# One weight matrix of a decode block loaded as two halves of its partitions, from two DMA queues

## The chip, the cores and the metric

The kernel runs on one core of a Trainium2 chip. A core has a matrix engine (TensorE, PE in the profile), a vector engine (VectorE, DVE), an engine for activation functions (ScalarE, ACT), a general engine (GpSimd, POOL) and one that mostly issues transfers (SyncE, SP). Sixteen DMA engines move data between the chip's main memory and the core's on-chip memory, which has 128 partitions. The metric is the time of one execution on the device in microseconds (us), as a median over runs; lower is better.

## What is computed

One decode step of a transformer block: a layer norm, then attention over a cache and a feed-forward layer beside each other, both added to the input. All data are 32-bit floats.

```python
B, Sq, D = 4, 1, 512
H, Sk, Dh = 32, 4096, 128        # F = 1792

def _A_ref(x, k_cache, v_cache, wq, wo):
    q = (x @ wq).reshape(B, Sq, H, Dh).transpose(0, 2, 1, 3)
    scores = jnp.einsum("bhqd,bhkd->bhqk", q, k_cache) * (Dh ** -0.5)
    p = _softmax(scores, axis=-1)
    o = jnp.einsum("bhqk,bhkd->bhqd", p, v_cache)
    return o.transpose(0, 2, 1, 3).reshape(B, Sq, H * Dh) @ wo

def _B_ref(x, w1, w2):
    h = _silu(jnp.einsum("bsd,df->bsf", x, w1))
    return jnp.einsum("bsf,fd->bsd", h, w2)

xn = _layernorm(x, axis=-1)
return x + _A_ref(xn, k_cache, v_cache, wq, wo) + _B_ref(xn, w1, w2)
```

The two caches are 4 x 32 x 4096 x 128 floats each, 268 MB apiece. wq is 512 x 4096 floats (8.39 MB), wo as large, w1 and w2 3.67 MB each.

## The kernel before

**Tiles and stages.** The caches are worked through in 32 tiles (`T`): one batch row and four heads at a time. A tile of K or V is 128 partitions x 128 rows x 128 floats, 64 KB in each partition, 8.39 MB in all. There are two buffers for K (`kb[0]`, `kb[1]`) and one for V (`v_t`).

**The start.** Before the first tile, w1 (line 196) and x (line 197) are loaded into `kb[0]`, wq (line 198) into `v_t`, and the first K tile, K(0), into `kb[1]` (line 199). The layer norm follows on x (lines 282 to 295, mostly DVE, the square root of line 288 on ScalarE), its transposes (lines 301 to 303), the first feed-forward product with w1 (line 312), the SiLU (line 322), its transposes into `hT` (lines 326 to 336), then the query product with wq: 64 matmuls recorded at line 348, whose first waits for wq's semaphore. Lines 359 to 371 rearrange the queries into `q_h`, and line 378 spreads them over the partitions.

**The loop.** For each tile DVE multiplies K by the spread queries (line 391) and, with GpSimd's help (line 422), sums the products into scores (lines 398 and 401); ScalarE takes exponentials (line 457); PE multiplies them with V (line 473); ScalarE copies the result out (line 466), GpSimd and PE gather it by heads (lines 431 to 439 and 483). After the last tile wo and w2 are multiplied in (lines 585 to 605), the result is copied and stored in two parts, one issued by SyncE and one by ScalarE (line 616).

**What sets the order.** The program is written out by hand: every engine has its own list of instructions, and semaphores order them. SyncE's list is one queue of loads: w1, x, wq, K(0), then K(1), which waits for the transposes of line 326 because `kb[0]` holds w1 and x until then, V(0), which waits for line 348 because `v_t` holds wq, and from there K(t+1) and V(t) in turn. K(t+1) waits for `k_free`, raised when the scores of two tiles before are done with the buffer, and V(t) for `v_free`, raised when PE has done with the V tile before. The last V tile goes into a K buffer; wo follows V in `v_t`, and w2 follows K in `kb[0]`. A DMA raises its semaphore by 16 when all of it has landed.

**Names that matter.** `load` (line 165) issues a load from SyncE, lets it raise a semaphore by 16 and gives back the pair of semaphore and count that a user waits for; `d_wq` is that pair for wq. The view `src` of wq puts four rows of the matrix, 64 KB, into each of the 128 partitions, and `wq_t` is the same shape in `v_t`.

Of the kernel before, what the change touches and what calls it, by code (L numbers as in the profile page):

```python
# [22 lines left out]
def kernel(  # L23
# [30 lines left out]
    P = nc.NUM_PARTITIONS  # L54
# [19 lines left out]
    PE, DVE, ACT, POOL, SP = nc.tensor, nc.vector, nc.scalar, nc.gpsimd, nc.sync  # L74
# [9 lines left out]
    sem = tc.alloc_semaphore  # L84
# [41 lines left out]
    wq_t = v_t.rearrange("p (c m) d -> p c (m d)", c=DC)  # L126
# [38 lines left out]
    def load(dst, src, s, *deps):  # L165
        inst = SP.dma_start(dst, src)
        for d, n in deps:
            inst.wait_op(d, n, "sem-ge", check=False)
        inst.then_inc(s, 16)
        return (s, 16)  # L170
# [19 lines left out]
    def load_k(t, *deps):  # L190
        load(kb[(t + 1) % 2], cache_tile(k_cache, t), k_landed[(t + 1) % 2], *deps)
# [3 lines left out]

    d_w1 = load(w1_t, w1.rearrange("(p c) f -> p c f", p=P), sem("w1"))
    d_x = load(x_sb, xf, sem("x"))
    d_wq = load(wq_t, wq.rearrange("(p c) n -> p c n", p=P), sem("wq"))
    load_k(0)


# [24 lines left out]
    rows = ident.rearrange("p (g n) -> p n g", g=G)  # L226
# [93 lines left out]
    for j in range(4):  # L320
        part_rows, n = slice(32 * j, 32 * j + B), FN[j] * P
# [20 lines left out]
    for m in range(NM):  # L342
        for c in range(DC):
            for j in range(4):
                n = NM * j + m
# [256 lines left out]
    for e, eng in enumerate((SP, ACT)):  # L602
# [9 lines left out]
        for k, j in enumerate((2 * e, 2 * e + 1)):  # L612
            c = acc[32 * j : 32 * j + B, :]
# [40 lines left out]
```

## Time and profile before

| | us |
|---|---|
| median of 3 runs | 1302.58 (1302.27 to 1302.63) |
| the profiled execution | 1302.57 |
| its span | 1300.8 |

| engine | busy us | share of the span |
|---|---|---|
| PE, matmuls | 401.0 | 31% |
| DVE | 912.0 | 70% |
| ACT | 99.8 | 8% |
| POOL | 576.4 | 44% |

The profile is one execution, taken by the hardware profiler. Its page gives busy times, the span in 40 slices of 32.5 us, the DMA queues, the chain of work that ended last, groups of instructions by source line, and DMA issues. A digit in a row of slices is the busy share in tenths, 9 meaning 90% or more; the rows "DMA" and "GB/s" are the mean busy share of the 16 DMA engines and what they moved. The timeline has one row for an instruction or a merged run of them: start, duration, engine, line, operation, output from input with shapes, count, and in brackets how long the engine had been idle and what released it. An engine's name with a q (SPq) is its sequencer, which issues DMAs and handles waits. The tensors are named by their buffers: `k<-in_B_w_dram` is w1 at the start (w2 at the end) going into a K buffer, `v<-in_A_wq_dram` is wq going into the V buffer. Windows give busy times, the granted TensorE clock, the DMA share and GB/s for chosen stretches of the span.

### The profile page before, as it was taken

What the parts mean: (1) busy time and instruction counts of PE and PEld (TensorE: products, weight loads), DVE (VectorE), ACT (ScalarE), POOL (GpSimd) and SP (SyncE); (2) the same over time, 40 slices, a digit from 0 to 9 for tenths busy, and PEclk for the clock granted to TensorE, in tenths of its full rate; (3) what the DMA queues carried; (4) which work ended last, traced back from release to release, by engine and by line L of the source; (5) the groups of instructions that cost most, each with busy time, mean ns of one, the idle gap of its engine ahead of it and who ended that gap; (6) DMA issues with size and microseconds to landing.
All of it is one profiled execution on the core that took longest, in us unless ns stands there. A gap on an engine that the chain in (4) does not pass through costs nothing. (4 is left out here: it accounts for less than half of the span.)

```text
span 1300.8 us, 6793 instructions
## 1 busy us (share of the span) xinstructions
PE 401.0 (31%) x2486; PEld 96.2 (7%) x2486; DVE 912.0 (70%) x324; ACT 99.8 (8%) x304; POOL 576.4 (44%) x220
## 2 busy tenths in 40 slices
PE   3322333321233331133332133332123333113337
PEld 1000000000000000000000000000000000000002
DVE  1488866877666787766687766687766678776670
ACT  1010001000010000100000000100001000000000
POOL 0155545544335545334554434554433554533450
PEclk9756666655666655666665666665566665566668
DMA  9999999999999999999999999999999999999998
GB/s 403 450 421 440 431 425 442 423 447 423 445 425 443 427 441 429 437 433 433 437 425 441 423 447 423 445 425 443 427 441 429 437 433 433 437 421 445 423 434 357
DMA packets 10543, 561.09 MB, mean 431 GB/s; under 512 B 1180, under 2 KB 1444, under 8 KB 1576
## 3 DMA queue, kind: packets, MB, share of 16 engines
q1 hardware_dynamic: 10528, 561.01, 99.6%
q8 instruction: 3, 0.05, 0.0%
q14 instruction: 4, 0.03, 0.0%
q10 hardware_dynamic: 8, 0.00, 0.0%
HBM read 561.00 MB, written 0.01 MB: 431 GB/s over the span
## 5 line engine op out<-in xcount | busy, mean ns | idle before, releaser
L422 POOL TENSOR_TENSOR k<-k 128x4096 f32<-128x4096 f32 x64 | 497.6, 7793 | 537.2 <-POOLq L173 537.2
L391 DVE TENSOR_TENSOR k<-k,q_ps 128x8192 f32<-128x8192 f32 x64 | 553.1, 8684 | 210.7 <-DVEq L173 210.6
L473 PE MATMUL o_ps<-v,p_t 128*16 128x512 f32 x1984 | 285.9, 741 | 751.3 <-PEq L173 751.3
L401 DVE TENSOR_REDUCE s<-k 128x64 f32<-128x4096 f32 x64 | 248.4, 3882 | 20.3 <-DVEq L173 20.3
L473 PEld LDWEIGHTS o_ps<-v,p_t 128*16 128x16 f32 x1984 | 67.4, 113 | 971.2 <-issue 971.2
L398 DVE TENSOR_REDUCE s<-k 128x16 f32<-128x2048 f32 x32 | 73.2, 2286 | 73.7 <-DVEq L173 73.7
L466 ACT ACTIVATE o_sb<-o_ps 128x512 f32<-128x512 f32 x31 | 18.5, 597 | 992.2 <-ACTq L173 992.2
L431 POOL TENSOR_TENSOR o_sb<-o_sb,own 128x512 f32<-128x512 f32 x31 | 32.2, 1039 | 107.7 <-POOLq L173 107.7
L457 ACT ACTIVATE p_t<-s,nb 32x128 f32<-32x128 f32 x128 | 66.0, 516 | 81.0 <-ACTq L173 79.4
L483 PE MATMUL o_all<-o,wsel 128*32 128x512 f32 x62 | 32.7, 608 | 88.2 <-PEq L173 88.2
L378 PE MATMUL q_ps<-q_h,spread 128*128 128x512 f32 x66 | 38.0, 659 | 26.9 <-PEq L173 26.0
L457 ACT ACTIVATION_READ_ACCUMULATOR p_t<-s,nb (+1 forms) x128 | 25.1, 196 | 0.0
L434 POOL TENSOR_TENSOR o_sb<-o_sb 128x256 f32<-128x256 f32 x31 | 22.4, 723 | 2.4
L233 POOL COPY wsel<-w_t 128x32 f32 (+1 forms) x8 | 1.7, 211 | 36.2 <-POOLq L173 36.2
L439 POOL TENSOR_TENSOR o<-o_sb 128x128 f32<-128x128 f32 x31 | 14.0, 453 | 1.1
L457 ACT ACT_TABLE_LOAD x7 | 9.0, 1283 | 70.0 <-ACTq L173 70.0
L378 PEld LDWEIGHTS q_ps<-q_h,spread 128*128 128x128 f32 x66 | 10.0, 191 | 54.4 <-issue 53.2
L483 PEld LDWEIGHTS o_all<-o,wsel 128*32 128x32 f32 x62 | 4.4, 108 | 113.0 <-issue 113.0
L405 DVE TENSOR_REDUCE m_t<-s 128x1 f32<-128x128 f32 x32 | 9.2, 287 | 4.7
L553 DVE TENSOR_TENSOR o_sb<-o_ps,own 128x512 f32<-128x512 f32 x1 | 0.7, 692 | 16.4 <-PE sm L560 16.4
L473 PE MATMUL o_ps<-k,p_t 128*16 128x512 f32 x64 | 9.5, 760 | 5.7 <-DMA k<-in_A_v_cache_dram 5.7
L413 DVE STREAM_TRANSPOSE nb<-gm 128x32 f32<-128x32 f32 x32 | 6.8, 211 | 6.0 <-DVEq L412 2.5
(87 smaller groups left out, 94.1 us busy)
## 6 DMA issues: line engine op xcount, KB each, us to landing
v<-in_A_wo_dram SPq DMA_DIRECT2D x2, 4096.0 KB, 24.5
k<-in_B_w_dram SPq DMA_DIRECT2D x1, 3584.0 KB, 11.3
k<-in_B_w_dram SPq DMA_DIRECT2D x1, 1792.0 KB, 32.0
k<-in_B_w_dram SPq DMA_DIRECT2D x1, 1024.0 KB, 34.1
k<-in_A_k_cache_dram SPq DMA_DIRECT2D x32, 46.8
k<-in_B_w_dram SPq DMA_DIRECT2D x1, 512.0 KB, 34.8
v<-in_A_v_cache_dram SPq DMA_DIRECT2D x31, 29.0
k<-in_B_w_dram SPq DMA_DIRECT2D x2, 128.0 KB, 34.6
```

Of the source, the lines that this page charges most:

```text
L378: return PE.matmul(q_ps.rearrange("p b d -> p (b d)"), spread.rearrange("p g i -> p (g i)"), q_h.rearrange("h b d -> h (b d)"), start=True ...
L391: DVE.tensor_tensor(k[:, a : a + STEP, :], k[:, a : a + STEP, :], q_ps[:, u : u + 1, :].to_broadcast([P, STEP, Dh]), op=ALU.mult,).then_in ...
L398: DVE.tensor_reduce(s[:, a + n : a + STEP], k[:, a + n : a + STEP, :], axis=AX, op=ALU.add)
L401: last = DVE.tensor_reduce(s[:, a : a + n], k[:, a : a + n, :half], axis=AX, op=ALU.add)
L422: POOL.tensor_tensor(k[:, a : a + n, :half], k[:, a : a + n, :half], k[:, a : a + n, half:], op=ALU.add).then_inc(halves, 1)
L431: POOL.tensor_tensor(o_sb, o_sb, own[:, :, None].to_broadcast([P, NR, Dh]), op=ALU.mult).then_inc(own_pool, 1)
L434: i = POOL.tensor_tensor(o_sb[:, :2, :], o_sb[:, :2, :], o_sb[:, 2:, :], op=ALU.add)
L439: POOL.tensor_tensor(o4[:, u, :], o_sb[:, 0, :], o_sb[:, 1, :], op=ALU.add).then_inc(heads_ready, 1)
L457: i = ACT.activation(p_t[rows, :, g], s[rows, :], AF.Exp, bias=nb[rows, :1], scale=-1.0, accum_out=l_t[rows, u, bass.ds(it, 1), g],)
L466: ACT.activation(o_sb, o_ps.rearrange("p (r d) -> p r d", r=NR), AF.Copy).then_inc(o_copied, 1)
L473: last = PE.matmul(o_ps[j : j + NR * G, :], p_t[:, rows, :].rearrange("p r g -> p (r g)"), v[:, rows, :].rearrange("p r d -> p (r d)"), st ...
L483: PE.matmul(o_all.rearrange("h b d -> h (b d)"), wsel, o4.rearrange("p b d -> p (b d)"), start=False, stop=False,)
```

## The change

The load of wq is split by partitions. Partitions 0 to 63 are loaded by a DMA that SyncE issues at the old place, between x and K(0); partitions 64 to 127 by a DMA that ScalarE issues, as the first instruction of its list. Both raise the same semaphore by 16, and the user of wq (line 348, four lines further down in the changed file) waits for 32. Nothing else is changed; all later lines move down by four.

```diff
@@ -195,7 +195,11 @@
 
     d_w1 = load(w1_t, w1.rearrange("(p c) f -> p c f", p=P), sem("w1"))
     d_x = load(x_sb, xf, sem("x"))
-    d_wq = load(wq_t, wq.rearrange("(p c) n -> p c n", p=P), sem("wq"))
+
+    d_wq = (sem("wq"), 32)
+    for eng, rows in ((SP, slice(0, P // 2)), (ACT, slice(P // 2, P))):
+        src = wq.rearrange("(p c) n -> p c n", p=P)
+        eng.dma_start(wq_t[rows], src[rows]).then_inc(d_wq[0], 16)
     load_k(0)
```

## The prediction

> **What bounds the kernel now.** I read the page's slices and queues first, then the DMA queue's own order of time, then the first 55 us of all engines, then the windows at both ends.
>
> ```profile
> span 1300.8 us, 6793 instructions
> DMA  9999999999999999999999999999999999999998
> GB/s 403 450 421 440 431 425 442 423 447 423 445 425 443 427 441 429 437 433 433 437 425 441 423 447 423 445 425 443 427 441 429 437 433 433 437 421 445 423 434 357
> DMA packets 10543, 561.09 MB, mean 431 GB/s; under 512 B 1180, under 2 KB 1444, under 8 KB 1576
> q1 hardware_dynamic: 10528, 561.01, 99.6%
> q10 hardware_dynamic: 8, 0.00, 0.0%
> ```
>
> Read here that the 16 DMA engines move data in 99.6% of the span, from the first slice to the last, nearly all of it for one queue (q1, the one that SyncE issues to). q10 carries 8 packets; its one customer is the output store that ScalarE issues. No compute engine comes near (DVE's digits are mostly 6 to 8), so the time is the bytes divided by the pace, and an edit counts only if it changes the pace or leaves the queue empty.
>
> The pace comes from the DMA queue in order of time, late in the loop, where each round loads one K and one V tile:
>
> ```profile
> 1144.80 0.33 SPq L166 DMA_DIRECT2D k<-in_A_k_cache_dram  x1
> 1182.53 0.33 SPq L166 DMA_DIRECT2D v<-in_A_v_cache_dram  x1
> 1183.39 0.33 SPq L166 DMA_DIRECT2D k<-in_A_k_cache_dram  x1
> 1220.65 0.33 SPq L166 DMA_DIRECT2D v<-in_A_v_cache_dram  x1
> 1221.99 0.33 SPq L166 DMA_DIRECT2D k<-in_A_v_cache_dram  x1
> ```
>
> From 1144.80 to 1183.39 and from there to 1221.99 is 38.60 us each. A tile is 128 x 16384 x 4 B = 8.39 MB, so 19.30 us per tile, 434.7 GB/s, 27.2 GB/s per DMA engine if they share evenly. The two rounds agree within 0.01 us: this is a fixed ceiling. wq has a tile's size, so it costs 19.30 us too, and w1 (128 x 7168 x 4 B = 3.67 MB) costs 8.44 us.
>
> The start, where the change sits (timeline; "<-" names what ended an idle time):
>
> ```profile
> 0.91 1.28 ACT L288 ACT_TABLE_LOAD   x1 [0.91 <-SPq L175]
> 0.96 0.38 SPq L166 DMA_DIRECT2D k<-in_B_w_dram  x1
> 1.40 0.37 SPq L166 DMA_DIRECT2D k<-in_A_x_dram  x1
> 1.81 0.35 SPq L166 DMA_DIRECT2D v<-in_A_wq_dram  x1
> ...
> 12.32 0.67 DVE L282 TENSOR_REDUCE nmean<-k 4x1 f32<-4x512 f32 x1 [7.92 <-DMA k<-in_A_x_dram]
> ...
> 15.31 0.20 ACT L288 ACTIVATE rstd<-var 4x1 f32<-4x1 f32 x1 [13.12 <-DVE var L287]
> ...
> 28.92 0.41 DVE L336 COPY hT<-sm 128x16 f32<-128x16 f32 x4 [11.00 <-PE sm L326]
> ...
> 31.70 8.60 PE L348 MATMUL sm<-v,xpad 128*32 128x512 f32 x64 [2.82 <-DMA v<-in_A_wq_dram]
> ...
> 40.43 0.33 SPq L166 DMA_DIRECT2D v<-in_A_v_cache_dram  x1
> ...
> 43.15 1.12 PE L378 MATMUL q_ps<-q_h,spread 128*128 128x512 f32 x2 [0.89 <-DVE q_h L371]
> ...
> 52.03 8.69 DVE L391 TENSOR_TENSOR k<-k,q_ps 128x8192 f32<-128x8192 f32 x1 [8.27 <-DVEq L173]
> ```
>
> w1, x, wq and K(0) stand in one queue in that order. x is there at 12.32, wq at 31.70; the scores of tile 0 start at 52.03, when K(0) is in: (3.67 + 8.39 + 8.39 MB) at 434.7 GB/s is 47.0 us, plus the start and the landing. The queries are ready at 43.15 + 1.12 = 44.27, 7.8 us earlier, so the small chain from x to the queries is covered by K(0)'s transfer.
>
> **The change, part by part.** *Issues.* SyncE still issues one wq transfer, of 64 partitions; ScalarE issues the other ahead of everything it does. An issue takes 0.35 to 0.38 us (the rows at 0.96 to 1.81). It pushes ScalarE's table load from 0.91 to about 1.3, ending near 2.6; ScalarE's first real work is at 15.31 and waits for data from DVE. Cost 0, cover 12.7 us; without that cover it would be 0.4 us. The one wait on wq (line 348) asks for 32 counts instead of 16, no instruction more. Sixteen more completion packets join 1180 small ones: nothing.
>
> *Order.* The upper half no longer stands behind w1 and x, but beside them in the other queue. So w1 and x are served more slowly. If everything of the upper half went ahead of x at the present pace, x would come 19.30 / 2 = 9.65 us later, at 21.97. From x to the end of hT are now 29.33 - 12.32 = 17.01 us, so hT would be ready at 38.98, and the 64 matmuls of line 348, next in PE's order, would start there, 7.3 us later than 31.70. The queries would end at 51.6, still ahead of K(0) at 52.03. The loads that hang on this chain are K(1) behind hT and V(0) behind line 348 (28.9 and 40.43 now):
>
> ```profile
> L166 SPq DMA_DIRECT2D k<-in_A_k_cache_dram x2: 328/464/599, 2.2 to 28.9; - x2
> 82.28 0.33 SPq L166 DMA_DIRECT2D k<-in_A_k_cache_dram  x1
> 100.59 0.33 SPq L166 DMA_DIRECT2D v<-in_A_v_cache_dram  x1
> ```
>
> K(1) would be issued at about 38.6, V(0) at 47.8; the queue has K(0) until 52 and K(1) until 71.3, so it doesn't run empty. Even if the first scores slipped, K(2) (issued at 82.28) has until V(0) is in, 71.3 + 19.3 = 90.6: 8.3 us of room. Order alone costs 0; the next thing late would be K(2), past 8.3 us.
>
> *The pace of a half.* This is the unknown. Every large load of the trace spans all 128 partitions, 8 to each DMA engine, so no row shows a transfer of 64. Bounds from the nearest rows: if the ceiling belongs to each engine's own work, a half moves at 434.7 GB/s and costs 9.65 us, the two together 19.30, as now: 0. If the ceiling belongs to the receiving side, so many bytes per group of partitions, 64 partitions take half the pace: 217 GB/s, 19.30 us for each half, 38.60 for both: +19.30 us. A gain in pace is excluded by the slices: the mean is 431 of 434.7.
>
> Between these ends I take the receiving side. The pace is the same for K and V, which come from different tensors, and no slice falls away from it where source rows change length (28 KB of w1, 64 KB of wq and the caches): that speaks against the source and for a limit at the end that all have in common. [...]
>
> [...]
>
> *Do the halves run together?* Under a receiving-side limit they would lose nothing if they did: one fills the lower groups, the other the upper ones. But the lower half stands behind w1 and x in SyncE's queue. Per engine w1 is 8 rows of 28 KB (8.44 / 8 = 1.06 us each), the upper half 4 rows of 64 KB (2.41 us at full, 4.83 at half pace). If an engine alternates rows of the two queues, four rounds take 4 x (1.06 + 4.83) = 23.5 us; the upper half is then done and four rows of w1 are left, 4.2 us. At 27.7 us w1 and x are through, and only now the lower half starts, alone: 19.3 us more, 47.0 in all against 8.44 + 19.30 = 27.74 now. The halves don't meet, and the full +19.30 falls due. x then comes at about 12.32 + 19.3 = 31.6, hT at 48.6, wq at 31.70 + 19.3 = 51.0: PE still waits for wq last, and the whole start, K(0) included, moves by 19.3.
>
> *Nothing gives it back.* The queue is full from K(0) to the end:
>
> ```profile
> 0.00:2.00 2.00, 0.00 (x0) 0.00 (x0) 0.80 (x3) 1.09 (x1) 1.18 (x8) 1.00 0.19 43
> 1240.00:1260.00 20.00, 9.93 (x66) 2.40 (x66) 16.92 (x4) 0.60 (x1) 15.60 (x4) 0.67 0.97 419
> 1260.00:1280.00 20.00, 10.74 (x74) 2.51 (x75) 3.19 (x9) 2.07 (x8) 1.90 (x4) 0.74 1.01 438
> 1280.00:1293.00 13.00, 11.47 (x78) 3.62 (x82) 1.00 (x3) 0.00 (x0) 0.00 (x0) 0.74 0.96 412
> ```
>
> (The last two columns are the DMA share and GB/s.) At 0.96 to 1.01 the tail has no idle DMA in which lost time could vanish. **Sum:** 0 (issues) + 0 (order) + 19.3 (pace of the halves) on the profiled execution's 1302.57 us (span 1300.8, 1.8 around it): 1321.9. The median of the runs is 1302.58, the same, so 1321.9 stands for it too.
>
> **The rivals.** *Engine-paced halves (not slower).* The mechanism is the lower bound: each DMA engine moves 27.2 GB/s wherever it writes. Place: wq's 8.39 MB; price 0; it decides as soon as a row of a half takes 2.41 us. For it: the engines' evenness suits it as well. Time 1302.6, within 0.5.
>
> *Halves that partly meet.* If w1 gets more than its alternate rows, the lower half starts while part of the upper still runs, and both run at full pace together. Were w1 first altogether, 8.44 us and then both halves at once in 19.30 would cost nothing; midway +9.65: 1312.2. Against it is only the count of rows above.
>
> *A quicker start.* The first 2 us hold a DMA share of 0.19, and slice one moves 403 instead of 431 GB/s: 28 x 32.5 us is 0.91 MB or 2.1 us at that pace. Two queues that filled all of it would give 1300.5. It is a bound, and below 0.2% (2.6 us, about what a measurement here can tell from no change).
>
> *The two queues don't run beside each other.* If the engines served ScalarE's half only when SyncE's queue is idle, it would wait behind K(0), and line 348 with it: hT and V(0) late, yet V(0)'s place in the stream would be taken by that half. At half pace this is again +19.3; at full pace line 348 starts at 52 instead of 31.70, the first scores some 20 us late, 20 - 8.3 = 12 us over the room that K(2) has: 1314.
>
> **How the numbers follow.** Receiving-side limit with halves apart: 0.66. Partly meeting: 0.13. Engine-paced: 0.15. Served late: 0.04. Quicker start: 0.02. The likeliest gives 1321.9. The range runs from 1308 (partly meeting, most of the way to free) to 1325 (19.3 plus up to 3 us if the first slice's shortfall of 2.1 us is paid once more); it leaves out the engine-paced and quicker-start cases, 0.17, and little else. Slower by over 0.2%: 0.66 + 0.13 + 0.04 = 0.83. Within 0.2%: 0.15 and the greater part of the quicker start, 0.16. Faster: 0.01.
>
> **What would show it.** In the profile after: slice one near 260 GB/s (w1 and the upper half, 7.86 MB, and 0.6 MB of the lower, in 32.5 us) instead of 403, the DMA digits still 9 (engines held up count as busy), q10 with 64 large packets; x at 20 to 32 us; the first line-391 product near 71 us; the same 38.60 us rounds after it. A first product still at 52 proves the engine-paced rival, one between 55 and 66 the partial meeting. My forecast is wrong if the start moves and the end doesn't, or if the rounds change.

## The result, and the profile after

| | before | after |
|---|---|---|
| median of 6 runs, us | 1302.42 | 1326.17 |
| range of the runs | 1302.17 to 1302.84 | 1325.69 to 1328.15 |
| the profiled execution, us | 1302.57 | 1326.30 |
| its span | 1300.8 | 1324.5 |

The changed kernel is 23.75 us slower: a ratio of 1.0184, 95% interval 1.0171 to 1.0197. The sign and the place were forecast, the size was not: 1321.9 was forecast, with a range up to 1325. Of the four executions of the eight eighths, in the experiments below, one took 1619.22 us at a lower granted clock (0.618 against 0.638 to 0.642), and its ratio leaves that one out.

The page of the profile after, in slices of 33.1 us and by DMA queue:

```profile
span 1324.5 us, 6794 instructions
DMA  9999999999999999999999999999999999999998
GB/s 238 286 441 443 426 429 440 435 426 441 435 431 431 439 435 426 441 433 431 433 439 433 428 441 433 426 439 439 433 428 439 435 426 439 439 431 429 439 426 355
q10 hardware_dynamic: 88, 4.20, 1.5%
```

Read the two DMA rows together. The digits are 9 from the first slice, as before, yet the first two slices move 238 and 286 GB/s where the kernel before moved 403 and 450. The engines were never without work; they were slow at it. From the third slice on both kernels run alike. Two slices short by 165 and 164 GB/s, 33.1 us each, are 10.9 MB, and at 434 GB/s that is 25 us: the loss and its place, within the roughness of slices. q10, ScalarE's queue, now carries half of wq.

The start, in the timeline after:

```profile
0.92 0.55 ACTq L202 DMA_DIRECT2D v<-in_A_wq_dram  x1
...
1.50 1.28 ACT L292 ACT_TABLE_LOAD   x1 [1.50 <-SPq L175]
...
1.82 0.56 SPq L202 DMA_DIRECT2D v<-in_A_wq_dram  x1
...
35.75 0.67 DVE L286 TENSOR_REDUCE nmean<-k 4x1 f32<-4x512 f32 x1 [31.34 <-DMA k<-in_A_x_dram]
...
55.95 8.62 PE L352 MATMUL sm<-v,xpad 128*32 128x512 f32 x64 [3.96 <-DMA v<-in_A_wq_dram]
...
76.30 17.29 DVE L395 TENSOR_TENSOR k<-k,q_ps 128x8192 f32<-128x8192 f32 x2 [8.27 <-DVEq L173]
```

x comes at 35.75 instead of 12.32 (+23.43), wq at 55.95 instead of 31.70 (+24.25), the first scores start at 76.30 instead of 52.03 (+24.27), and the execution ends 23.73 later. So everything is lost before x arrives but for 0.8 us, and 0.5 us come back by the end. The wait ahead of the first scores is 8.27 us in both kernels: the chain to the queries stays as well covered as it was.

One view more, of single packets, tells what happened between 2 and 55 us. A packet here is one partition's row, 28 KB of w1 or 64 KB of wq or K; 16 of them are under way at any moment from 6 to 30 us, as many as there are DMA engines. The table is made from the packet records of the trace, taken 16 at a time in order of their starts: each line is read as one row on each of the 16 engines, which the records don't name, with the time of one packet (the eighth of the 16 by length).

```
first start, last end, bytes,  queue, median us of a packet
 1.97   5.80   28672  q1   first two rows of w1, one after the other (1.07 the second)
 4.79  10.81   65536  q10  4.6
 9.26  12.48   28672  q1   1.9
11.30  17.47   65536  q10  4.8
15.93  19.07   28672  q1   1.9
17.91  24.03   65536  q10  4.7
22.53  25.61   28672  q1   1.9
24.49  30.55   65536  q10  4.7
29.08  31.83   28672  q1   1.7
31.04  34.29   28672  q1   1.06 (the last two rows of w1)
33.18  39.62   65536  q1   4.8   (the lower half, four rows)
37.85  44.73   65536  q1   5.13
42.97  49.85   65536  q1   5.13
48.09  54.88   65536  q1   5.13
53.23  57.54   65536  q1   3.2   (K(0), first row; the next ones 2.42)
```

A 64 KB row takes 2.42 us in K(0) and 5.13 in a half that is alone; the queues take turns row by row, and w1's rows take 1.7 to 1.9 us between rows of the half, against 1.06 alone.

### The profile page after: what moved, and what is told of

Read it like the earlier page. It is cut to its first block, busy times and chain, and to the rows that moved or that the text cites. A ratio compares the mean times of both kernels' runs of the same rounds, so it can differ in the third digit from the quotient of the medians.

```text
span 1324.5 us, 6794 instructions
## 1 busy us (share of the span) xinstructions
PE 399.7 (30%) x2486; PEld 95.5 (7%) x2486; DVE 912.0 (69%) x324; ACT 99.8 (8%) x304; POOL 576.7 (44%) x220
## 6 DMA issues: line engine op xcount, KB each, us to landing
k<-in_B_w_dram SPq DMA_DIRECT2D x1, 1792.0 KB, 31.6
```

## The experiments

Each differs from the kernel before only at the load of wq, and was run over several rounds against the kernel before on the same chip (medians there between 1302.49 and 1302.84). The cuts of code show the lines that matter, with ... for lines left out; the count that the user of wq waits for is 16 for each piece.

| experiment | median us | ratio to before, 95% interval |
|---|---|---|
| both halves in SyncE's queue | 1323.79 | 1.0162 (1.0145 to 1.0179) |
| halves by columns, two queues | 1302.48 | 0.9998 (0.9988 to 1.0007) |
| wq whole, in ScalarE's queue | 1307.01 | 1.0033 (1.0020 to 1.0045) |
| both halves ahead of w1, two queues | 1326.83 | 1.0186 (1.0169 to 1.0203) |
| four quarters, SyncE | 1324.26 | 1.0166 (1.0149 to 1.0183) |
| eight eighths, SyncE | 1356.61 | 1.0413 (1.0393 to 1.0434) |
| 32 to 95, then 0 to 31, then 96 to 127, SyncE | 1313.46 | 1.0082 (1.0065 to 1.0098) |
| the change, upper half after x | 1323.22 | 1.0158 (1.0142 to 1.0175) |
| 32 to 95 from ScalarE, the rest SyncE | 1313.66 | 1.0084 (1.0067 to 1.0101) |

**The halves or the queues?** Two kernels split the change. The first keeps the halves and gives both to SyncE:

```diff
+    for eng, rows in ((SP, slice(0, P // 2)), (SP, slice(P // 2, P))):
```

> Both halves stand in SyncE's queue, one after the other; ScalarE issues none. If the loss belongs to the halves themselves (two DMA engines share the receiving side of each group of partitions, about 20.5 us a half as in the second half of the changed kernel), wq takes 41.0 us instead of 19.3: 1302.4 + 21.7 = 1324.1, with x back at 12.3 us. If it belongs to serving two queues at once: 1302.4.

The second keeps the two queues and halves the columns instead:

```diff
+    for eng, cols in ((SP, slice(0, DC // 2)), (ACT, slice(DC // 2, DC))):
...
+        eng.dma_start(wq_t[:, cols], src[:, cols]).then_inc(d_wq[0], 16)
```

> Two queues as in the change, but each half is half of the columns of all 128 partitions (32 KB of each partition's 64 KB). If the loss belongs to the halves of partitions: 1302.4 within 1 us, x at about 12.3 + 9.65 = 22 us, covered. If it belongs to serving two queues at once: about 1326 as in the change.

Both came out on the side of the halves: 21.1 us slower (1323.79 against 1302.72), and no change (1302.48). The timeline of the first:

```profile
12.51 0.67 DVE L285 TENSOR_REDUCE nmean<-k 4x1 f32<-4x512 f32 x1 [8.11 <-DMA k<-in_A_x_dram]
...
53.48 9.94 PE L351 MATMUL sm<-v,xpad 128*32 128x512 f32 x64 [24.75 <-DMA v<-in_A_wq_dram]
```

and one window of it, whose last two columns are DMA share and GB/s (a window counts a packet whole where it starts, so with rows of about 5 us both are rough at a window's edges, in a short window the most):

```profile
14.00:50.00 36.00, 8.87 (x44) 2.75 (x44) 3.27 (x15) 3.62 (x6) 0.00 (x0) 0.70 0.99 204
```

x is early again, and from x to wq the queue needs 40.97 us where the kernel before needed 31.70 - 12.32 = 19.38. A window with a DMA share of 0.99 at 204 GB/s is what these two halves look like, one after the other: busy, at 0.47 of 434.

The second's window at the start, and its x and first scores:

```profile
4.00:28.00 24.00, 1.98 (x19) 0.84 (x22) 4.51 (x16) 1.49 (x2) 0.00 (x0) 1.00 0.99 428
```

```profile
21.74 0.67 DVE L285 TENSOR_REDUCE nmean<-k 4x1 f32<-4x512 f32 x1 [17.33 <-DMA k<-in_A_x_dram]
...
51.97 17.29 DVE L394 TENSOR_TENSOR k<-k,q_ps 128x8192 f32<-128x8192 f32 x2 [1.87 <-DVEq L173]
```

Two queues at full pace, 428 GB/s. x is 9.42 us late, as half of wq went ahead of it, and the wait before the first scores shrinks from 8.27 to 1.87 us: covered, so nothing is seen at the end.

**A whole wq beside w1.**

```diff
+    for eng, rows in ((ACT, slice(0, P)),):
```

> The whole of wq, 128 partitions, in ScalarE's queue beside w1, x and K(0) in SyncE's. Partition-half theory: no loss of pace; w1's 8 rows per engine alternate with 8 rows of wq, so x comes at 29 to 32 us, hT near 48, the queries near 60, the first scores 8 us later than before, which is about the room that K(2) has: 1302.4 to 1304. Two-queue theory: twice the changed kernel's time in company of another queue, 1326 or more.

Measured: 1307.01, 4.3 us slower, above what was expected. The pace is not to blame; the room of K(2) is. Its timeline and two windows:

```profile
31.41 0.67 DVE L285 TENSOR_REDUCE nmean<-k 4x1 f32<-4x512 f32 x1 [27.01 <-DMA k<-in_A_x_dram]
...
61.99 17.29 DVE L394 TENSOR_TENSOR k<-k,q_ps 128x8192 f32<-128x8192 f32 x2 [0.66 <-DVEq L173]
...
92.23 0.33 SPq L166 DMA_DIRECT2D k<-in_A_k_cache_dram  x1
```

```profile
4.00:29.00 25.00, 0.04 (x1) 0.00 (x0) 0.25 (x2) 0.00 (x0) 0.00 (x0) 1.00 0.97 422
88.00:96.00 8.00, 0.00 (x0) 0.00 (x0) 7.59 (x7) 2.35 (x6) 0.00 (x0) 0.50 0.45 156
```

w1 and wq side by side move 422 GB/s: whole rows in turn cost nothing. But x is 19 us late, the first scores 9.96, K(2)'s issue 9.95 (92.23 against 82.28), and from 88 to 96 the DMA share is 0.45. By the packet records the first engine runs out of V(0) at 89.0, the engines stand idle for 3.7 us each on average, and K(2)'s first packets start at 93.19 to 93.95, against 88.52 to 90.01 in the kernel before: 3.9 to 4.7 us late, which is the loss of the median. (The profiled execution, at 1308.35 the slowest of the six, lost 5.8; where its other 1 to 2 us went isn't known.) The room was thus about 5.5 us (9.95 less some 4.4), not the 8.3 of the forecast. That one let the queue last until 90.6 and K(2) be issued then; in the kernel before the first engines turn to K(2) at 88.52 already, and a packet starts 1.0 to 1.7 us after the issue.

**Would the halves help each other if they met?** The lower half goes first in SyncE's queue:

```diff
+    for eng, rows in ((SP, slice(0, P // 2)), (ACT, slice(P // 2, P))):
...
+        eng.dma_start(wq_t[rows], src[rows]).then_inc(d_wq[0], 16)
     d_w1 = load(w1_t, w1.rearrange("(p c) f -> p c f", p=P), sem("w1"))
```

> The lower half is put first in SyncE's queue, ahead of w1, so that both halves run from the first moment and w1 beside neither. If the engines alternate rows in step, all 16 on the same half at a time: both halves 41.0 us, 1302.4 + 21.7 = 1324.1. If the halves complement each other when they meet (one half of the engines on the lower, the other on the upper groups): 19.3 us for both, 1302.4, with x and the chain behind it late by up to 19.3 us, of which 8 fit into cover and 8 into K(2)'s room: 1302.4 to 1306.

Measured: 1326.83, 24.1 us slower. The windows:

```profile
6.00:40.00 34.00, 0.00 (x0) 0.00 (x0) 0.00 (x0) 0.00 (x0) 0.00 (x0) 1.00 1.02 216
100.00:106.00 6.00, 0.65 (x1) 0.00 (x0) 3.79 (x2) 0.00 (x0) 5.52 (x1) 0.50 0.83 360
106.00:114.00 8.00, 0.00 (x0) 0.00 (x0) 7.59 (x7) 1.33 (x2) 0.00 (x0) 0.50 0.69 262
```

With both halves in flight from the first moment the window has 216 GB/s, hardly more than the 204 of one half at a time; by the packet records a row takes 4.96 us instead of 5.13. They don't complement each other: in the same records 16 packets of the upper half start, then 16 of the lower, in turn. The two later windows hold 6 x 0.17 + 8 x 0.31 = 3.5 us of idle DMA (3.2 by the packet records), which the expectation of 1324.1 had left out: x, behind both halves and w1, is so late that K(2) misses its time, as in the experiment before.

**What sets the pace of a part?** Three kernels with SyncE's queue alone:

```diff
+    for eng, rows in ((SP, slice(a, a + 32)) for a in range(0, P, 32)):
```

> wq as four transfers of 32 partitions, all in SyncE's queue. [...] If the pace goes with the number of partitions: quarter pace, 77 to 82 us, 1360 to 1365.

```diff
+    for eng, rows in ((SP, slice(a, a + 16)) for a in range(0, P, 16)):
```

> wq as eight transfers of 16 partitions, all in SyncE's queue. [...] If any transfer below 128 partitions just goes at half pace: 1324.

```diff
+    for eng, rows in ((SP, slice(32, 96)), (SP, slice(0, 32)), (SP, slice(96, P))):
```

> wq as partitions 32 to 95 in one transfer, then 0 to 31, then 96 to 127, all in SyncE's queue. [...] If 64 partitions are slow wherever they lie: 20.5 + 2 x 10.25 = 41.0 us, 1324.1. [...]

Quarters cost what halves cost (21.4 us), eighths 53.8 us, and the split with the middle 10.6 us, half of the loss. From x to wq in the timelines, eighths first, then the middle:

```profile
12.41 0.67 DVE L285 TENSOR_REDUCE nmean<-k 4x1 f32<-4x512 f32 x1 [8.01 <-DMA k<-in_A_x_dram]
...
85.86 8.39 PE L351 MATMUL sm<-v,xpad 128*32 128x512 f32 x64 [56.41 <-DMA v<-in_A_wq_dram]
```

```profile
12.04 0.67 DVE L285 TENSOR_REDUCE nmean<-k 4x1 f32<-4x512 f32 x1 [7.63 <-DMA k<-in_A_x_dram]
...
42.88 8.83 PE L351 MATMUL sm<-v,xpad 128*32 128x512 f32 x64 [14.63 <-DMA v<-in_A_wq_dram]
```

That is 73.45 us, 114 GB/s, and 30.84 us. 64 partitions from 32 to 95 go at full pace (2.42 us a row in the packet records), 64 from 0 to 63 at half (5.13 in the changed kernel). So neither the number of partitions nor the split as such sets the pace; nor does the source, as both are 64 neighbouring rows of the same matrix. What is left is which partitions are written: the same row of 64 KB takes 2.42 us in 32 to 95, 5.13 in a half and 9.1 in sixteen neighbours (73.45 us for eight such transfers). By what mechanism these differ was not shown.

**Why 23.75 and not 21?** The change, with ScalarE's half held until x is there:

```diff
+        i = eng.dma_start(wq_t[rows], src[rows])
+        if eng is ACT:
+            i.wait_op(*d_x, "sem-ge", check=False)
...
```

> The change, but ScalarE's half waits until x has landed, so that its rows alternate with the lower half's and not with w1's. If what the change loses beyond the halves' own pace (23.8 against 21.1 us with both halves in one queue) comes from rows of w1 moving beside a half, it goes away: wq at 20.1 to 21.3 us more than before (4.96 us a row where halves alternated, 5.13 where they followed each other), 1322.5 to 1324. If it comes from having two queues at work at all: 1326.

And the middle in ScalarE's queue beside w1:

```diff
+    for eng, rows in ((SP, slice(0, 32)), (SP, slice(96, P)), (ACT, slice(32, 96))):
```

> Partitions 32 to 95 in ScalarE's queue beside w1; 0 to 31 and 96 to 127 in SyncE's. [...] If a half beside w1 costs its 2 to 3 us wherever it lies: 1316.

1323.22 is 20.7 us over before, so the extra went away; 1313.66 is the time of the three pieces in one queue (1313.46). The windows of w1's stretch in each, first the upper half after x, then the middle beside w1:

```profile
4.00:11.00 7.00, 0.04 (x1) 0.00 (x0) 0.26 (x2) 0.00 (x0) 0.00 (x0) 1.00 0.97 418
```

```profile
4.00:19.00 15.00, 0.04 (x1) 0.00 (x0) 0.26 (x2) 0.00 (x0) 0.00 (x0) 1.00 1.01 436
```

w1 beside the middle moves at the full 436 GB/s in two queues; beside the upper half, in the changed kernel, the window from 6 to 30 us has 203 (227 by the packets' own times, with no engine idle; the share of 0.89 comes from the window's edges):

```profile
6.00:30.00 24.00, 0.00 (x0) 0.00 (x0) 0.00 (x0) 0.00 (x0) 0.00 (x0) 1.00 0.89 203
```

So the extra 2 to 3 us are rows of w1 that move between rows of a half. That this is so is shown by taking either away: by the packet records a row of w1 takes 1.06 us both with the upper half held back and beside the middle, once the first row is through. In the changed kernel the engines finish a row of the half up to 1.5 us apart (9.26 to 10.81 us for the first); how the longer rows of w1 come about was not shown.

## Why the prediction was right or wrong

*What bounds the kernel:* right. The rounds after the start are as before, and a loss of DMA time at the start comes out at the end nearly whole (24.27 us at the first scores, 23.73 at the end). How the tail gave back half a microsecond isn't known.

*Issues:* right in being free, but an issue of 64 partitions took 0.55 us, not 0.35, and moved the table load to 1.50, not 1.3; the first ScalarE work that needs it starts at 38.74, so nothing came of it.

*Order:* right for this kernel, where K(0) is late too; in columns x was 9.42 us late and covered, as worked out with 9.65. The room of K(2) was put at 8.3 us and is about 5.5; it entered no sum, but cost two expectations about 3 us each.

*The pace of a half:* the first of two terms that were too small, and together they are the failed step. The upper bound was the right choice of the two: in the runs the pace goes with the partitions that are written (2.42 us a row in 32 to 95, 5.13 in a half). That a limit of so many bytes per group of partitions is behind it was the author's reading, and no run shows such groups. The bound was taken as exactly half the pace, 19.30 us for each half and +19.30 in all. Measured with both halves in one queue, the two need 40.97 us from x to wq instead of 19.38, and the kernel 21.1 us more: a half moves at 204 GB/s, not 217. That is the first missing 2 us.

*Do the halves run together:* the order was right, row by row, w1 done after the upper half and the lower half alone after it. The four rounds were priced at 4 x (1.06 + 4.83) = 23.5 us with w1 at its own pace; they took 26.2 (4.79 to 31.04 in the packet table), as w1's rows took 1.7 to 1.9 us there. x came at 35.75, not 31.6, and outside the 20 to 32 named as its sign. That is the second missing 2 to 3 us. Neither term alone passes 1325: 1321.9 + 1.8 is 1323.7, and 1321.9 + 2.7 is 1324.6; only both together do. Within the changed kernel itself the account is 2.7 us more in the four rounds, 0.75 in the lower half (33.18 to 53.23, 20.05 us for 19.3) and 0.8 in the first row of K(0) behind it (3.2 for 2.42), 4.25 in all, and 4.3 are missing. The side remark that halves would lose nothing if they met is wrong as well: they take 4.96 us a row, and in the packet records 16 rows of one half go, then 16 of the other.

*The rivals:* engine-paced halves fell with both halves in one queue; partly meeting halves with both ahead of w1; the two queues not running beside each other with x at 35.75, and with 428 GB/s for the columns; a quicker start with 1302.48 there.

## What to carry to other kernels

A DMA digit of 9 doesn't say that the pace is the ceiling (here it stood at 238 GB/s in the first slice and at 441 in the third): read it with the GB/s beside it, and look for stretches that are busy at half the rate. Where DMA is the bound, split a transfer along columns, not partitions (1302.48 against 1326.17 us); in these runs the lower or the upper half of the partitions took about as long as all 128 or a little more (20.05 us for the lower half, 19.30 for all), from whichever queue, while partitions 32 to 95 took half of that (four rows of 2.42 us). In these runs a second queue gave no pace to a queue that was already full (428 GB/s with the columns in two queues); it only changed who came first (x was 9.42 us late there), so ask what stands behind in the other queue.

## What was not expected of the hardware

- In the lower or the upper half of the partitions, one after the other, a row moved at less than half the pace: 5.13 us for 64 KB against 2 x 2.42. In sixteen neighbouring partitions a row took 9.1 us, less than 4 x 2.42; a run of eighths moved 114 GB/s where a quarter of 434 is 108.5.
- The queues took turns in whole rows (16 rows of the half, then 16 of w1, in the packet table): x was 9.42 us late behind 32 KB rows of half of wq and 19.1 us behind 64 KB rows of all of it, so the queue with the longer rows got the larger share.
- An issue took 0.55 to 0.61 us for 64 partitions in one block, and 0.35 to 0.41 us for half of the columns of 128.
